# Fourier mixing and softmax attention on one core: the first product of a chain without its wait, and one reciprocal per full block of row sums

## The chip, the cores and the metric

The kernel runs on one core of one Trainium2 chip. The metric is the device time of one execution in microseconds (us); lower is better. One execution was also taken by the hardware profiler, and all lines below that come from the trace belong to that one.

## What is computed

The input `x` has 2048 rows of 512. The result mixes two things row by row with a gate `g = sigmoid(sum(x * gate_w))`:

```
a = Cr @ (x @ Hr.T) - Ci @ (x @ Hi.T)          # Fourier part, dense matrices: 2048x2048 and 512x512
p = softmax(q @ k.T * scale)                    # 32 heads of 16, 2048 x 2048 scores each
b = (p @ v) @ wo
out = g * a + (1 - g) * b
```

Here `q`, `k`, `v` come from a second input by one projection. All is float32. The kernel splits an operand into a high and a low part and makes three products (high·high, high·low, low·high) where one would lose accuracy.

## The kernel before, in words

**Stages.** (1) Projections for `q`, `k`, `v` and the imaginary hidden transform, whole array (128 rows). (2) One long stage in which attention and the Fourier part run side by side. (3) A tail: the last attention units, the last output projections and stores.

**Two streams side by side in stage 2.** The TensorE array has 128 rows. A matmul of the Fourier part (a "product", `Chain.mm`, L339 to L345) contracts over 128, but in this stage it is cut in two halves of 64 rows. While one half of the array computes a product, the other half computes a score matmul, since a score contracts over only 48 or 50 rows (16 per head, times three parts, and two rows that carry the negated maximum). So the list of products is issued twice per pair of segments: once for `half=0` and once for `half=1`, both adding into the same PSUM tile `d`.

- Score matmuls are of two kinds. An "a" score (`a_tile`, L198; matmul at L204) is made to find the row maximum: VectorE reduces it (L206). An "s" score (`scores`, L621; matmul at L629) is made transposed and goes through the exponential on ScalarE (L630) into a tile `pt`. Each kind has three PSUM buffers (`psA`, `psS`), so the fourth score of a kind waits until the first has been consumed.
- "Value" products (`pv`, L632; matmul at L638) multiply `pt` with `v` into the PSUM tile `acc`: four matmuls per unit, 17 columns each, in four column groups of the array. They need the exponentials of both heads of the unit. There are 512 units (16 head pairs x 32); row 16 of each group holds the sum of the exponentials.

**Chains.** A chain (`Chain`, L332) is all products that add into one tile `d`. There is one PSUM buffer for `d` in this stage (`psD`), so a new chain's first product must also wait until the chain before has been evacuated: ScalarE copies it at L359 (chains of 12, the real hidden transform), L397 or L400 (chains of 48, the sequence transform), or VectorE finishes it at L521 (chains of 9, the output projection). The evacuation is issued right behind the last product of the second half.

**Order of the work.** It is written out by hand. `pairs` (L764) yields pairs of segments, and `segment` (L738) walks through a pattern string. A slot of one letter issues one product, then one score of that kind on the other half of the array. A slot of two letters issues two scores and no product. A bar issues one unit of values. The patterns are

```python
FULL = "a s a s a s s a s a s a s a s a | |"
THIN = "aS s s a a s a | a s a a s s sA |"
NINE = "sA s s a a sA | a a s a s aS |", "aS a s s a aS | sA a s a s s sA |"
```

There are 13 pairs of THIN (12 products each, one chain per pair), 96 pairs of FULL (16 products each, one chain in three pairs) and 13 pairs of NINE (9 products each, one chain per pair). Ahead of them three chains are run with the whole array.

**The wait that is touched.** `users` collects who consumes each score issued since the last product of a segment (an exponential for "s", a reduction for "a"). At the next segment's start the list becomes `before`, and the first product of that segment gets a wait (L754) on the latest "s" consumer in it, or, if there is none, on the first entry. A FULL segment ends with one "a", so the next waits for its reduction. A THIN or NINE segment ends with scores of both kinds, so the next waits for its last exponential. The first pair of THIN starts with an empty list.

**Row sums.** Eight blocks (`hf` 0 or 1, `ct` 0 to 3) of up to four head pairs are normalised in passing. `sums` (L438) loads the sums of the exponentials from DRAM into `rc`, head 0 in partitions 0 to 63 and head 1 in 64 to 127, 64 elements in each; `inverse` (L446), put by the plan some units later, takes the reciprocals on VectorE (L450) and stores each half to DRAM (L451); `load_o` (L453) reads them back spread over rows. Seven blocks are full (`n` = 4); the block `hf` 1, `ct` 3 has three pairs. `run_plan` calls these ahead of a segment, so on each engine they stand in the queue ahead of that segment's work.

Of the kernel before, what the change touches and what calls it, by code (L numbers as in the profile page):

```python
# [31 lines left out]
def mix_kernel(ctx: ExitStack, tc: tile.TileContext, xa_t, xa, wqkv, w_hid, w_seq, wo, gate_w, out):  # L32
# [5 lines left out]
    nc = tc.nc  # L38
# [406 lines left out]

    def inverse(hf, ct, n=4):  # L446
        rc = rcs.pop((hf, ct))
        for h in range(2):
            rows = rc[64 * h:64 * h + 16 * n]
            nc.vector.reciprocal(rows, rows)  # L450
            nc.sync.dma_start(r_d[hf][ct][h, :n].rearrange("p (c f) -> c p f", f=64), rows)  # L451

    def load_o(o, sm, hf, ct, q0, n=4):  # L453
# [205 lines left out]
    def issue(x, half, stop=True):  # L659
        chain, st, mv, after, last = x  # L660
        i = chain.mm(st, mv, half, last and stop)
        if stop and after:
            after()
        return i
# [15 lines left out]
    for hf in range(2):  # L680
        for ct in range(4):
            n = 3 if hf and ct == 3 else 4
            last = 32 * (4 * ct + n - 1) + 16 * (hf + 1)
            at(last + (4 if ct < 3 else 2), sums, hf, ct, n)
            at(last + (12 if ct < 3 else 4), inverse, hf, ct, n)
            if ct < 3:
                for half in range(2):
                    for step, du in enumerate((16, 20, 22)):
                        at(last + du + 8 * half, block, step, hf, ct, half)
# [38 lines left out]
    def score(kind, h):  # L728
        x = next(streams[h][kind == "a"], None)
        if x:  # L730
            users.append((kind, (a_tile if kind == "a" else scores)(*x)))

    def values():
        nonlocal valued
        pv(valued)
        valued += 1

    def segment(pattern, half, ds, stop):  # L738


        nonlocal users
        before, users = users, []
        ds = iter(ds)
        for slot in pattern.split():
            if slot == "|":
                values()
                continue
            if len(slot) == 1:
                x = next(ds, None)
                if x:  # L750
                    i = issue(x, half, stop)
                    users = []
                    if before:
                        tc.add_manual_dep(  # L754
                            i.ins, dict(before).get("s", before[0][1]).ins.name,
                            mybir.DependencyInfo(mybir.DependencyClass.Sync, mybir.DependencyReason.DATA))
                        before = None
            score(slot[0], 1 - half)
            if len(slot) == 2:
                score(slot[1].lower(), half)  # L760
        if deferred:
            deferred.pop(0)()
# [29 lines left out]
    for patterns, ds in pairs():  # L792
        for half in range(2):
            run_plan(valued)
            segment(patterns[half], half, ds, half == 1)
# [59 lines left out]
```

## Time and profile before

| what | value |
|---|---|
| times of 3 runs | 1752.32 to 1754.02 us, median 1752.51 us |
| the profiled execution: its own time | 1753.26 us |
| the profiled execution: span from first to last instruction | 1751.5 us |
| mean granted TensorE clock in it | 0.995 |
| busy share: TensorE matmuls, VectorE, ScalarE, GpSimd | 99%, 78%, 66%, 26% |

In the lines of the profile PE is the matmul side of TensorE and PEld its weight loads; DVE is VectorE, ACT is ScalarE, POOL is GpSimd, SPq the queue of SyncE, which issues most DMAs. A timeline row gives the start in us from the span's start, the length in us, the engine, the source line, the operation, "output<-inputs", the shapes, and how many such instructions are merged in the row; in brackets stands how long the engine had been idle before it and what released it. Matmuls overlap: the length of one is longer than its distance to the next. A row of waits gives the total in us, the number of waits and the longest.

### The profile page before, as it was taken

To read this page: it belongs to the slowest core of one execution; us is meant where nothing else is said; L and a number is where in the kernel's file an instruction comes from. 1 tells how busy PE (TensorE), PEld (TensorE's weight loads), DVE (VectorE), ACT (ScalarE), POOL (GpSimd) and SP (SyncE) were. 2 spreads that over 40 slices of the span, in tenths; PEclk is the share of its full clock that TensorE was granted. 3 is DMA by queue.
4 is the path that set the end of the run, shared out by engine and by line. 5 is a ranking of instruction groups with operands and counts; after the bars stand their busy time and mean duration, and the time that the engine had idled before them with its cause. 6 is when DMAs were issued, how large, how long until landed. Compare 5 with 4: busy or idle time off the path is not lost.

```text
span 1751.5 us, 32890 instructions
## 1 busy us (share of the span) xinstructions
PE 1727.6 (99%) x12721; PEld 1042.1 (59%) x12721; DVE 1368.1 (78%) x2302; ACT 1153.6 (66%) x2257; POOL 447.0 (26%) x561
## 2 busy tenths in 40 slices
PE   8999999999999999999999999999999999999998
PEld 7886554456666666656666666666666566544443
DVE  5228878888888888888888888888888888899953
ACT  5211267776776777776767777767767777777776
POOL 0110222232223233222223243333323333200111
PEclk9999899999999999999999999999999999999999
DMA  8754630304133152414146443314141535461113
GB/s 291 234 113 138 224 42 7 56 21 78 44 62 67 45 123 80 86 55 79 38 80 211 107 127 98 72 57 86 44 85 56 129 98 98 146 168 26 38 27 127
DMA packets 82348, 164.79 MB, mean 94 GB/s; under 512 B 19712, under 2 KB 19968, under 8 KB 78352
## 3 DMA queue, kind: packets, MB, share of 16 engines
q1 hardware_dynamic: 77840, 162.30, 36.4%
q8 instruction: 100, 1.64, 0.4%
q0 software_dynamic: 4352, 0.39, 0.3%
q14 instruction: 56, 0.46, 0.1%
HBM read 107.47 MB, written 54.52 MB: 92 GB/s over the span
## 4 chain that ended last, share of the span: by engine, by line
PE 93%; DVE 2%; ACT 2%; DMA 1%; issue 0%; DVEq 0%; SPq 0%; ACTq 0%
PE d L343 35%; PE acc L638 26%; PE s L629 11%; PE a L204 11%; PE s L79 2%; PE s L80 2%; PE s L81 2%; DVE mx L206 1%; ACT pt L630 1%; DMA b<-hl 1%; PE a L79 1%; PE a L80 1%; PE a L81 1%; ACT y L359 0%; DVE hl L76 0%
## 5 line engine op out<-in xcount | busy, mean ns | idle before, releaser
L206 DVE TENSOR_REDUCE mx<-a 128x1 f32<-128x512 f32 x2026 | 1244.4, 681 | 243.3 <-PE a L204 229.5
L630 ACT ACTIVATE pt<-s 128x512 f32<-128x512 f32 x2008 | 1025.5, 622 | 391.2 <-PE s L629 333.7
L204 PE MATMUL a<-ks,qs 48*128 48x512 f32 x2026 | 814.4, 418 | 3.1 <-DVE mx L206 2.4
L629 PE MATMUL s<-qs,ks 50*128 50x512 f32 x2008 | 769.7, 413 | 0.9 <-ACT pt L630 0.8
L343 PE MATMUL d<-xab,ch 64*128 64x512 f32 x2016 | 648.7, 396 | 0.0
L638 PE MATMUL acc<-pt,vt 128*17 128x512 f32 x4096 | 500.3, 596 | 0.0
L343 PEld LDWEIGHTS d<-xab,ch 64*128 64x128 f32 x2016 | 365.9, 184 | 126.3 <-DVE mx L206 60.4
L629 PEld LDWEIGHTS s<-qs,ks 50*128 50x128 f32 x2008 | 365.6, 184 | 109.1 <-ACT pt L630 30.8
L204 PEld LDWEIGHTS a<-ks,qs 48*128 48x128 f32 x2026 | 366.8, 185 | 77.2 <-DVE mx L206 48.4
L343 PE MATMUL d<-xab,cl 64*128 64x512 f32 x1008 | 399.5, 396 | 0.0
L343 PEld LDWEIGHTS d<-xab,cl 64*128 64x128 f32 x1008 | 185.5, 184 | 64.9 <-DVE mx L206 40.8
L327 POOL CAST ch<-craw 128x512 fp32r<-128x512 f32 x126 | 77.1, 612 | 555.2 <-PE a L204 177.6
L638 PEld LDWEIGHTS acc<-pt,vt 128*17 128x17 f32 x4096 | 90.1, 96 | 206.0 <-issue 206.0
L328 POOL TENSOR_TENSOR cl<-craw,ch 128x512 fp32r<-128x512 f32 x126 | 162.1, 1287 | 10.2
L227 POOL DMA_DIRECT2D qs<-mt x128 | 72.0, 568 | 160.1 <-DVE mt L223 151.6
L343 PE MATMUL d<-wre,xab 64*128 64x512 f32 (+1 forms) x348 | 95.1, 406 | 5.0 <-ACT pt L630 2.5
L343 PEld LDWEIGHTS d<-wre,xab 64*128 64x128 f32 (+1 forms) x348 | 59.9, 185 | 42.6 <-issue 26.1
L343 PE MATMUL d<-wo_hl,o_hl 64*128 64x512 f32 (+1 forms) x261 | 71.0, 398 | 0.0
L343 PEld LDWEIGHTS d<-wo_hl,o_hl 64*128 64x128 f32 (+1 forms) x261 | 47.1, 185 | 15.9 <-issue 11.7
L75 ACT CAST hl<-s 128x512 fp32r<-128x512 f32 x32 | 18.7, 585 | 56.8 <-PE s L81 49.5
L76 DVE TENSOR_TENSOR hl<-s,hl 128x512 fp32r<-128x512 f32 x32 | 22.0, 687 | 35.0 <-ACT hl L75 35.0
L218 POOL CAST nhl<-nm 128x16 fp32r<-128x16 f32 x32 | 6.3, 197 | 151.2 <-DVE nm L215 151.2
(125 smaller groups left out, 931.8 us busy)
## 6 DMA issues: line engine op xcount, KB each, us to landing
craw<-w_seq SPq DMA_DIRECT2D x128, 256.0 KB
qk<-hl SPq DMA_DIRECT2D x32, 512.0 KB
qs<-qk SPq DMA_DIRECT2D x96, 128.0 KB
ks<-qk SPq DMA_DIRECT2D x96, 128.0 KB
b<-hl SPq DMA_DIRECT2D x16, 512.0 KB
xab<-b SPq DMA_DIRECT2D x16, 512.0 KB
o<-oe SPq DMA_DIRECT2D x62, 128.0 KB
oh<-nh SPq DMA_DIRECT2D x12, 512.0 KB
```

Of the source, the lines that this page charges most:

```text
L79: nc.tensor.matmul(ps, sh, mh, start=first, stop=False)
L80: nc.tensor.matmul(ps, sh, ml, start=False, stop=False)
L81: nc.tensor.matmul(ps, sl, mh, start=False, stop=last)
L204: nc.tensor.matmul(ps, qs[p % 2][r, qt * P:(qt + 1) * P], ks[p % 2][r, kb * 512:(kb + 1) * 512], start=True, stop=True)
L206: user = nc.vector.tensor_reduce(mx[p % 2][:, h, qt, kb:kb + 1], ps, AX.X, ALU.max)
L227: (nc.sync, nc.gpsimd)[h].dma_start(rows.rearrange("v (q b c) -> v b q c", q=8, b=4)[:, b], mt[hf][32 * b + h:32 * b + 32:2])
L327: nc.gpsimd.tensor_copy(h1, raw)
L328: nc.gpsimd.tensor_tensor(l1, raw, h1.bitcast(F32), ALU.subtract)
L343: i = nc.tensor.matmul(self.ps, st[r], mv[r], start=not self.begun, stop=stop)
L629: nc.tensor.matmul(ps, ks[p % 2][rr, kt * P:(kt + 1) * P], qs[p % 2][rr, q0:q0 + 512], start=True, stop=True)
L630: return nc.scalar.activation(pts[u][:, 2 * qb + h], ps, AF.Exp, bias=0.0, scale=DH ** -0.5)
L638: nc.tensor.matmul(acc[32 * j:32 * j + 17], vt[:, kt, p, 16 * h:16 * h + 17], pt[:, j], start=kt == 0, stop=kt == NT - 1)
```

## The change

Two edits. In `segment`, the list `before` is dropped when the product about to be issued is the first of its chain (`x[0].begun` is still false), so that product gets no wait on a score's consumer. Since the list is looked at only for the first product of a segment, this concerns segments in which a chain begins; the second segment of each pair, and the FULL pairs in the middle of a chain, keep their wait. In `inverse`, a full block takes one reciprocal over all 128 partitions of `rc` instead of two over 64 each; the block with three pairs keeps two operations. The two stores stay as they are.

```diff
     def inverse(hf, ct, n=4):
         rc = rcs.pop((hf, ct))
+        if n == 4:
+            nc.vector.reciprocal(rc, rc)
         for h in range(2):
             rows = rc[64 * h:64 * h + 16 * n]
-            nc.vector.reciprocal(rows, rows)
+            if n < 4:
+                nc.vector.reciprocal(rows, rows)
             nc.sync.dma_start(r_d[hf][ct][h, :n].rearrange("p (c f) -> c p f", f=64), rows)
...
                 x = next(ds, None)
                 if x:
+
+                    before = before if x[0].begun else None
                     i = issue(x, half, stop)
                     users = []
                     if before:
```

## The prediction

> **What bounds the kernel now.** First the page: the shares of the chain that ended last, by engine.
>
> ```profile
> PE 93%; DVE 2%; ACT 2%; DMA 1%; issue 0%; DVEq 0%; SPq 0%; ACTq 0%
> ```
>
> TensorE holds 93% of the chain. An edit that leaves TensorE's order of work alone can save only what TensorE stands still for, and the change takes away waits of TensorE. So the second view is the table of stages, here THIN's and FULL's (columns: window, length, PE busy, PEld, DVE, ACT, POOL, clock, DMA share, GB/s).
>
> ```profile
> 217.00:389.00 172.00, 169.38 (x1220) 83.84 (x1220) 141.70 (x233) 125.53 (x240) 40.24 (x53) 1.00 0.20 33
> 389.00:1532.00 1143.00, 1141.74 (x9208) 705.00 (x9212) 947.62 (x1597) 811.39 (x1606) 352.64 (x437) 1.00 0.36 86
> ```
>
> TensorE lacks 2.6 us of full in THIN's stage and 1.3 us in FULL's. There is little to win. The third view is who waited: matmuls, then weight loads.
>
> ```profile
> PE d L343 <- ACT pt L630: 3.3, 13, 0.7
> PEld d L343 <- DVE mx L206: 102.1, 120, 0.9
> PEld d L343 <- issue: 54.1, 66, 2.8
> ```
>
> The first row is a real stop: 13 times the array ran dry before a product, released by an exponential. The second looks far larger, 102 us, and is the trap of this profile: the weight load path also "waits" as long where nothing releases it (third row), as the next part shows.
>
> **The change, part by part.** From the loops, a chain begins 13 times in THIN, 32 times in FULL, 13 times in NINE; the first THIN start has no wait to lose. So 57 waits go: 12 THIN, the first FULL start (behind THIN), 31 FULL, 13 NINE.
>
> *31 FULL starts.* One of them, with what stands before it:
>
> ```profile
> 424.07 0.77 ACT L397 ACTIVATE y<-d,g 128x512 f32<-128x512 f32 x1
> 424.18 0.68 DVE L206 TENSOR_REDUCE mx<-a 128x1 f32<-128x512 f32 x1
> 424.41 1.04 PE L638 MATMUL acc<-pt,vt 128*17 128x512 f32 x8
> 425.38 0.50 PE L343 MATMUL d<-xab,ch 64*128 64x512 f32 x1
> 425.39 0.50 PE L204 MATMUL a<-ks,qs 48*128 48x512 f32 x1
> ```
>
> The removed wait is on the reduction that ends at 424.86; the product starts at 425.38, 0.52 us later and 0.97 us after the last eight value products began. A segment's middle, where this wait never was:
>
> ```profile
> 349.09 1.05 PE L638 MATMUL acc<-pt,vt 128*17 128x512 f32 x8
> 350.07 0.18 PEld L343 LDWEIGHTS d<-wre,xab 64*128 64x128 f32 x1 [0.85 <-issue]
> 350.07 0.50 PE L343 MATMUL d<-wre,xab 64*128 64x512 f32 x1
> 350.41 0.39 PE L343 MATMUL d<-wre,xab 64*128 64x512 f32 x1
> ```
>
> Again 0.98 us, with 0.85 us "idle" on the load path and nothing to release it. So the step from values to products costs the same with or without the wait: the value products hide it, with 0.52 us to spare, and I cost these 31 at nothing. The evacuation also ends at 424.84, no later than the reduction. If the cover were gone (value products half a microsecond shorter), the reduction would bind.
>
> *13 NINE starts.* Here a pair of scores comes first and the product second:
>
> ```profile
> 1600.19 1.05 PE L638 MATMUL acc<-pt,vt 128*17 128x512 f32 x8
> 1601.17 0.50 PE L629 MATMUL s<-qs,ks 50*128 50x512 f32 x1
> 1601.52 0.40 PE L343 MATMUL d<-wo_hl,o_hl 64*128 64x512 f32 x1
> ```
>
> The scores come 0.98 us after the values, the product 0.35 us after them. The unhindered second slot above is 350.41 − 350.07 = 0.34 us behind the first. Nothing to win.
>
> *12 THIN starts.* Same pattern, but the product is late:
>
> ```profile
> 351.36 0.39 PE L629 MATMUL s<-qs,ks 50*128 50x512 f32 x1
> 351.59 0.47 PE L629 MATMUL s<-qs,ks 50*128 50x512 f32 x1
> 352.97 0.49 PE L204 MATMUL a<-ks,qs 48*128 48x512 f32 x1
> 353.69 0.49 PE L343 MATMUL d<-wre,xab 64*128 64x512 f32 x1 [0.22 <-ACT pt L630]
> 354.02 0.39 PE L343 MATMUL d<-wre,xab 64*128 64x512 f32 x1
> 355.28 1.12 PE L638 MATMUL acc<-pt,vt 128*17 128x512 f32 x8
> ```
>
> 0.72 us instead of 0.34: 0.38 us late. ScalarE in the same stretch:
>
> ```profile
> 352.06 0.58 ACT L359 COPY y<-d 128x512 f32<-128x512 f32 x1
> 352.53 1.11 ACT L630 ACTIVATE pt<-s 128x512 f32<-128x512 f32 x2
> 353.02 1.12 ACT L630 ACTIVATE pt<-s 128x512 f32<-128x512 f32 x2
> 354.23 1.08 ACT L630 ACTIVATE pt<-s 128x512 f32<-128x512 f32 x2
> ```
>
> (The second and third row share one exponential.) The evacuation pushes the exponentials of the scores at 351.36 and 351.59 back; the second ends at 352.53 + 1.11 = 353.64, and the product starts right behind. Without the wait it goes at 352.97 + 0.34 = 353.31, since `d` is free at 352.64; the score beside it needs the buffer of the one at 351.36, free at about 353.14, and goes along. What is late next? The second score needs the buffer of the one at 351.59, free at 353.64. It takes the place that the first score has today, so the score stream gains one slot, 354.02 − 353.69 less the 0.10 us longer first step, 0.23 us. And the values at 355.28 need the exponentials of these two scores, which end at 354.23 + 1.08 = 355.31 today; the eight values then take 1.12 us instead of 1.05, so they already wait for them. ScalarE starts queued exponentials 0.49 us apart (352.53, 353.02), and each lasts 1.11 − 0.49 = 0.62. The third began 0.62 before its end at 354.14, at 353.52; the fourth, now at 354.23, could follow 0.50 later, at 354.02. ScalarE gives 0.20 us, and I take that: 12 x 0.20 = 2.4 us. Bounds: 0, if more of ScalarE's backlog comes back than I see, and the whole 0.38 us, 4.6 us in all. A loss is excluded by the queue's order, which stays, unless rival (4) holds.
>
> *The first FULL start*, behind THIN:
>
> ```profile
> 387.93 1.05 PE L638 MATMUL acc<-pt,vt 128*17 128x512 f32 x8
> 388.00 0.58 ACT L359 COPY y<-d 128x512 f32<-128x512 f32 x1
> 389.71 0.47 PE L343 MATMUL d<-xab,chl 64*128 64x512 f32 x1 [0.73 <-ACT pt L630]
> ```
>
> Unhindered it is 387.93 + 0.98 = 388.91, with `d` free at 388.58. That is 0.8 us. Its partner is an "a", and reductions are not behind; the next "s" comes a slot later and needs a buffer that has been freed long before. I take 0.8 us, between 0 and 0.8.
>
> *Reciprocals.* VectorE, with the shapes that bear on the price:
>
> ```profile
> L450 DVE RECIPROCAL rc<-rc 64x64 f32<-64x64 f32 x14 | 7.4, 529 | 3.0 <-DMA rc<-o 2.7
> L450 DVE RECIPROCAL rc<-rc 48x64 f32<-48x64 f32 x2 | 1.1, 542 | 0.0
> ```
>
> 48 partitions cost no less than 64 do, so the price goes by the elements per partition, and one over 128x64 is taken at 0.53 us; the other bound is twice that, what the two cost now. Two in one FULL segment show as
>
> ```profile
> 592.51 3.68 DVE L206 TENSOR_REDUCE mx<-a 128x1 f32<-128x512 f32 x6 [0.94 <-PE a L204]
> 597.42 1.08 DVE L450 RECIPROCAL rc<-rc 64x64 f32<-64x64 f32 x2
> 598.54 4.87 DVE L206 TENSOR_REDUCE mx<-a 128x1 f32<-128x512 f32 x8
> 604.48 1.89 DVE L206 TENSOR_REDUCE mx<-a 128x1 f32<-128x512 f32 x3 [1.07 <-PE a L204]
> ```
>
> From 592.51 to 598.54 are 6.03 us, from there to 604.48 are 5.94, the usual segment: VectorE has about 1.0 us of room in a segment, and the pair overruns it by 0.09. One operation fits. By the plan six of the seven full blocks fall into FULL: 6 x 0.09 = 0.5 us, between 0 and 0.5. The seventh falls into the tail. There one operation waits for both loads, and the first store goes out after it, some 0.7 us later than now:
>
> ```profile
> 1705.49 1.24 DVE L450 RECIPROCAL rc<-rc 64x64 f32<-64x64 f32 x2 [2.66 <-DMA rc<-o]
> 1719.23 1.23 DVE L488 TENSOR_TENSOR o_l<-o_raw,o_l 128x1024 fp32r<-128x1024 f32 x1
> 1724.55 0.50 PE L343 MATMUL d<-wo_hl,o_l 128*128 128x512 f32 x1
> ```
>
> In SP's queue these stores are followed by the reads of the same sums, which wait for them anyway. What is made of them is ready at 1720.46 and used first at 1724.55: 4.1 us of slack for 0.7. Nothing.
>
> **Sum:** 2.4 + 0.8 + 0.5 = 3.7 us. The profiled execution took 1753.26 us around its span of 1751.5, so 1749.6; the median of the runs is 0.75 us below the profiled one: 1752.51 − 3.7 = **1748.8 us**, 0.21% less. A measurement of this kernel can tell about 0.2% (3.5 us) from no change, so my forecast lies on that line.
>
> **The rivals.**
> (1) *TensorE keeps all it gains in THIN*: exponentials come sooner than I think and the 0.38 us stay, 2.2 us more off (12 x 0.18), 1746.6. For it: ScalarE is busy 73% of that stage. Against: the values' 1.12 us.
> (2) *FULL starts gain too*: the first product's weights load under the value products once nothing holds it, and its 0.50 us shrink to 0.39: 31 x 0.11 = 3.4 us more off, 1745.4. Against: at 350.07, without a wait, the load still starts with its product. The Trainium skill, "TensorE: Matmul & The Clock Gate", Step-by-step: what each phase is for, says that TensorE pulls weight loads ahead of running matmuls when the row groups don't conflict or a background buffer takes them; by that rule this rival would hold, and the row at 350.07 speaks against it at this place.
> (3) *THIN gives it all back* to ScalarE before the pair ends: 0.8 + 0.5 = 1.3 us, 1751.2.
> (4) *The starts lose step* (slower): the wait kept product and score side by side. If the score's buffer comes free over one slot (0.23 us) after the product, the product runs alone, and at the 31 FULL and 13 NINE starts a slot is lost: 44 x 0.23 = 10.1, less the 3.7: 6.4 us above the median, 1758.9. Against: the "a" at 425.39 leaves with its product, and its buffer was freed two reductions before 424.86.
> (5) *Nothing changes*, because the release of `d` holds the product anyway: 1752.5. Against: 352.64 and 388.58 are well before the products.
>
> **How the numbers follow.** Forecast 0.61, (1) 0.12, (2) 0.07, (3) 0.10, (4) 0.08, (5) 0.02. The forecast's half beyond the line is 0.31, so faster by over 0.2% is 0.31 + 0.12 + 0.07 = 0.50, within it 0.30 + 0.10 + 0.02 = 0.42, slower 0.08. The range takes in the bounds of THIN (0 to 4.6), of the first FULL start and of the reciprocals, so it reaches from rival (1) to a little past rival (3): 1746.6 to 1751.8. It leaves out (2), (4) and (5), 0.17.
>
> **What would show it.** In the changed profile the row of matmul waits for an exponential should fall from 13 to about one or none; a THIN start should put its product 0.34 us behind the first scores, with the second score held until an exponential ends; the values behind it should come about 0.2 us sooner; the first FULL product should come 0.98 us after the eight values; the other FULL starts should keep 0.97 us; segments with a reciprocal should last 5.94 us. I am wrong if FULL's usual segment changes its length, if a product at a chain's start runs without its score, or if the tail stretches.

## The result, and the profile after

Over 20 runs of each kernel the changed kernel took 1751.03 us (median; 1748.23 to 1755.13) and the kernel before 1753.76 us. The ratio is 0.998, with a 95% interval from 0.9973 to 0.9987. So the change gains 0.2% by this ratio, and 2.7 us (0.16%) between the medians; the forecast's line of 0.2% lies inside the interval. The forecast had 3.7 us off. The time forecast, 1748.8 us, lies 2.2 us below the one measured; 1.25 us of that is the kernel before, whose median in these 20 runs is that much above the 1752.51 us from which the forecast started.

The profiled execution after spans 1748.6 us (1751.5 before) and took 1750.4 us around it. First the chain of work that ended last, and from the waits of matmuls one row that is new (who waited for whom, total in us, times, longest):

```profile
PE 95%; DVE 2%; DMA 1%; ACT 1%; issue 0%; POOL 0%; DVEq 0%; SPq 0%; ACTq 0%; POOLq 0%
```

```profile
PE s L632 <- DMA qs<-mt: 1.2, 1, 1.2
```

TensorE's share of the chain rose from 93% to 95%. The row of 13 products that waited for an exponential, 3.3 us, is gone; the new row comes up again below. (Scores, exponentials and values now stand at L632, L633 and L641.) What is not gone with it shows only in the lengths of segments, so all that follows measures from a segment's first product to the next one's.

*THIN starts.* A start in the profile after, TensorE and ScalarE together:

```profile
350.16 3.08 ACT L633 ACTIVATE pt<-s 128x512 f32<-128x512 f32 x6
350.61 0.73 PE L632 MATMUL s<-qs,ks 50*128 50x512 f32 x2
350.95 0.64 PE L343 MATMUL d<-wre,xab 64*128 64x512 f32 x2
351.32 0.50 PE L632 MATMUL s<-qs,ks 50*128 50x512 f32 x1
352.68 1.16 PE L641 MATMUL acc<-pt,vt 128*17 128x512 f32 x8
```

The product follows the scores by 350.95 − 350.61 = 0.34 us, where it was 0.72. The values follow them by 2.07 us, where it was 355.28 − 352.97 = 2.31; the eight values then last 0.04 us longer. The first products of the second and the thirteenth THIN pair, before and then after, are eleven pairs apart:

```profile
245.79 0.50 PE L343 MATMUL d<-wre,xab 64*128 64x512 f32 x1 [0.20 <-ACT pt L630]
...
377.66 0.49 PE L343 MATMUL d<-wre,xab 64*128 64x512 f32 x1 [0.21 <-ACT pt L630]
```

```profile
244.87 0.64 PE L343 MATMUL d<-wre,xab 64*128 64x512 f32 x2
...
374.53 0.64 PE L343 MATMUL d<-wre,xab 64*128 64x512 f32 x2
```

131.87 / 11 = 11.99 us a pair became 129.66 / 11 = 11.79, so 0.20 us a start.

*First FULL start.* It comes 0.98 us after the eight values, as anywhere else:

```profile
384.98 1.05 PE L641 MATMUL acc<-pt,vt 128*17 128x512 f32 x8
385.96 0.49 PE L343 MATMUL d<-xab,chl 64*128 64x512 f32 x1
```

*A reciprocal in FULL.* VectorE after:

```profile
593.81 0.51 DVE L449 RECIPROCAL rc<-rc 128x64 f32<-128x64 f32 x1
594.84 4.88 DVE L206 TENSOR_REDUCE mx<-a 128x1 f32<-128x512 f32 x8 [0.52 <-PE a L204]
```

One operation over 128 partitions takes 0.51 us, and VectorE now stands idle 0.52 us before the next reduction. The six segments concerned last 5.943 us on the mean, 6.032 before.

*The other FULL starts.* This is where the forecast put nothing. One segment in which a chain begins, before (its first product starts at 425.38, a row of the prediction) and then after, with the loads on PEld:

```profile
425.93 4.87 DVE L206 TENSOR_REDUCE mx<-a 128x1 f32<-128x512 f32 x8 [1.07 <-PE a L204]
429.06 0.18 PEld L204 LDWEIGHTS a<-ks,qs 48*128 48x128 f32 x1
429.49 1.91 PE L638 MATMUL acc<-pt,vt 128*17 128x512 f32 x16
431.33 0.50 PE L343 MATMUL d<-xab,ch 64*128 64x512 f32 x1
```

```profile
421.64 0.50 PE L343 MATMUL d<-xab,ch 64*128 64x512 f32 x1
422.21 4.88 DVE L206 TENSOR_REDUCE mx<-a 128x1 f32<-128x512 f32 x8 [1.09 <-PE a L204]
425.35 0.18 PEld L204 LDWEIGHTS a<-ks,qs 48*128 48x128 f32 x1
425.78 1.91 PE L641 MATMUL acc<-pt,vt 128*17 128x512 f32 x16
427.62 0.50 PE L343 MATMUL d<-xab,ch 64*128 64x512 f32 x1
```

From the first product to the first reduction: 0.55 us before, 0.57 after. To the last "a" load: 3.68 and 3.71. To the values: 4.11 and 4.14. To the next segment: 5.95 and 5.98. The segment is 0.025 us longer (medians 5.947 and 5.971 us over 30 chain starts; the segments in which no chain begins stay at 5.947).

*Where the 2.9 us between the two spans come from*, each as a difference of distances between first products:

| stretch | change, us |
|---|---|
| up to THIN's first product (233.53 to 232.96; no edit there) | −0.57 |
| 12 THIN starts | −2.36 |
| first FULL start (last THIN half 6.24 to 5.42) | −0.82 |
| six segments behind a reciprocal, 6 x 0.089 | −0.53 |
| 30 other FULL starts (their sum 178.44 to 179.16) | +0.72 |
| four segments at FULL's end (24.96 to 25.61) | +0.65 |
| rest of FULL | +0.17 |
| NINE (150.69 to 150.65) and tail (67.42 to 67.35) | −0.11 |

The +0.65 sits at one score, after and then before:

```profile
1508.57 0.47 PE L632 MATMUL s<-qs,ks 50*128 50x512 f32 x1 [1.22 <-DMA qs<-mt]
```

```profile
1511.31 0.47 PE L629 MATMUL s<-qs,ks 50*128 50x512 f32 x1 [0.55 <-ACT pt L630]
```

It waits for a small transfer of the negated maxima, whose last part GpSimd issues at 1503.30 us. In the eleven further kernels below, these four segments last between 24.66 and 25.59 us with no order by the edits: the kernel with all of the wait edit and nothing else has 24.87. I read it as scatter of that transfer between executions, not as an effect of the change.

### The profile page after: what moved, and what is told of

Its sections match the earlier page's. It is cut to its first block, busy times and chain, and to the rows that moved or that the text cites. A ratio compares the mean times of both kernels' runs of the same rounds, so it can differ in the third digit from the quotient of the medians.

```text
span 1748.6 us, 32869 instructions
## 1 busy us (share of the span) xinstructions
PE 1726.6 (99%) x12721; PEld 1041.4 (60%) x12721; DVE 1364.2 (78%) x2295; ACT 1152.2 (66%) x2257; POOL 447.9 (26%) x561
## 4 chain that ended last, share of the span: by engine, by line
PE 95%; DVE 2%; DMA 1%; ACT 1%; issue 0%; POOL 0%; DVEq 0%; SPq 0%; ACTq 0%; POOLq 0%
PE d L343 34%; PE acc L641 27%; PE a L204 12%; PE s L632 12%; PE s L79 2%; PE s L80 2%; PE s L81 2%; DVE mx L206 1%; PE a L79 1%; PE a L80 1%; PE a L81 1%; DMA b<-hl 1%; ACT pt L633 0%; PE a L343 0%; DMA qs<-mt 0%
## 5 line engine op out<-in xcount | busy, mean ns | idle before, releaser
L633 ACT ACTIVATE pt<-s 128x512 f32<-128x512 f32 x2008 | 1024.1, 620 | 390.0 <-PE s L632 342.3
L632 PE MATMUL s<-qs,ks 50*128 50x512 f32 x2008 | 769.9, 413 | 1.5 <-DMA qs<-mt 1.2
L641 PE MATMUL acc<-pt,vt 128*17 128x512 f32 x4096 | 500.7, 596 | 0.0
L632 PEld LDWEIGHTS s<-qs,ks 50*128 50x128 f32 x2008 | 366.1, 184 | 112.0 <-ACT pt L633 33.6
L641 PEld LDWEIGHTS acc<-pt,vt 128*17 128x17 f32 x4096 | 90.6, 96 | 205.8 <-issue 205.7
```

The costliest lines, as they stand in the source:

```text
L632: nc.tensor.matmul(ps, ks[p % 2][rr, kt * P:(kt + 1) * P], qs[p % 2][rr, q0:q0 + 512], start=True, stop=True)
L633: return nc.scalar.activation(pts[u][:, 2 * qb + h], ps, AF.Exp, bias=0.0, scale=DH ** -0.5)
L641: nc.tensor.matmul(acc[32 * j:32 * j + 17], vt[:, kt, p, 16 * h:16 * h + 17], pt[:, j], start=kt == 0, stop=kt == NT - 1)
```

## The experiments

The theory from these profiles: dropping the wait gains 0.20 us at each THIN start and 0.8 us at the first FULL start, and loses 0.025 us at every other FULL start. Rivals: the longer FULL segments come from the reciprocal edit or from a drift of the work, or from the moment at which the product starts. A loss of 0.7 us is under what whole runs can tell, so the segment lengths decide; the ratios stand beside them. All figures in us; 5.947 is a segment with no chain start.

| kernel | THIN pair | last THIN half | chain start in FULL | behind a reciprocal | NINE | ratio, 95% interval |
|---|---|---|---|---|---|---|
| before | 11.988 | 6.241 | 5.947 | 6.032 | 150.69 | |
| after | 11.788 | 5.420 | 5.971 | 5.943 | 150.65 | 0.998, 0.9973 to 0.9987 |
| wait edit alone | 11.788 | 5.417 | 5.971 | 6.029 | 150.69 | 0.9995, 0.9986 to 1.0005 |
| reciprocal alone | 11.989 | 6.230 | 5.946 | 5.946 | 150.69 | 0.9997, 0.9987 to 1.0006 |
| FULL starts keep the wait | 11.786 | 5.434 | 5.946 | 5.943 | 150.64 | 0.9981, 0.9972 to 0.9991 |
| FULL starts alone lose it | 11.980 | 6.220 | 5.971 | 6.031 | 150.62 | 1.0009, 0.9995 to 1.0023 |
| earlier reduction | 11.789 | 5.416 | 5.944 | 5.943 | 150.76 | 0.998, 0.9969 to 0.999 |
| evacuation on VectorE | 11.796 | 5.632 | 5.970 | 5.944 | 150.64 | 0.9986, 0.9977 to 0.9995 |
| one reciprocal for three pairs | 11.792 | 5.417 | 5.945 | 5.945 | 149.90 | 0.9987, 0.9978 to 0.9995 |
| score first | 11.798 | 5.420 | 5.932 | 5.944 | 150.63 | 0.9986, 0.9977 to 0.9996 |
| later values | 12.036 | 5.431 | 5.970 | 5.944 | 150.67 | 1.0009, 0.9999 to 1.0019 |
| score first, three pairs | 11.787 | 5.417 | 5.933 | 5.945 | 149.90 | 0.9981, 0.9972 to 0.999 |
| the same with later values | 12.037 | 5.430 | 5.935 | 5.946 | 149.82 | 1.0, 0.9991 to 1.0008 |

"Last THIN half" is the distance from the last THIN half's first product to FULL's first.

**The wait edit alone**, on the kernel before:

```diff
                 if x:
+                    before = before if x[0].begun else None
                     i = issue(x, half, stop)
```

> The wait dropped at all chain starts, the two reciprocals kept as before. Theory A: the edit gains 12 x 0.20 us at the THIN starts and 0.8 us at the first FULL start, and loses about 0.025 us at each of 31 FULL starts, since the first product now signals its own end ahead of its score and the first reduction starts later; so 2.4 us less than before, a FULL segment that begins a chain lasts 5.972 us, the others 5.947, and the six segments with two reciprocals stay at 6.03. Rival B: the longer chain-start segments have to do with the reciprocal edit or are drift; then they last 5.947 here and the gain is 3.2 us.

The span was 1749.1 us. THIN and the first FULL start gain as in the changed kernel and the other FULL starts lose as in it. One of them:

```profile
422.29 0.50 PE L343 MATMUL d<-xab,ch 64*128 64x512 f32 x1
422.86 4.88 DVE L206 TENSOR_REDUCE mx<-a 128x1 f32<-128x512 f32 x8 [1.09 <-PE a L204]
428.27 0.50 PE L343 MATMUL d<-xab,ch 64*128 64x512 f32 x1
```

Again 0.57 us to the first reduction and 5.98 us in all. Segments behind a reciprocal keep their 6.03 us. So the loss does not come from the reciprocals.

**The reciprocal alone**, the change without its second edit:

```diff
-                    before = before if x[0].begun else None
                     i = issue(x, half, stop)
```

> The waits kept as before, one reciprocal per full block. Theory A: six segments lose 0.09 us each, 0.5 us in all, too little for the times to tell; a FULL segment that begins a chain lasts 5.947 us like the others. Rival B: those segments last 5.972 us here. Rival C: the tail or the stores of the sums pay something back, and the stage behind FULL gets longer by a few tenths of a us.

Only the six segments move. The span of 1753.8 us is longer than before's; 3.0 us of that lie ahead of THIN (236.57 against 233.53), where nothing was edited. The last section comes back to this stretch.

**FULL starts keep the wait.** The change, but a list without an "s" is kept:

```diff
-                    before = before if x[0].begun else None
+                    before = before if x[0].begun or "s" not in dict(before or ()) else None
```

> The change, but the wait stays where it is on a reduction (31 FULL starts and the first NINE start). Theory A: the gains stay and the loss goes: 2.4 + 0.8 + 0.5 = 3.7 us less than before, 0.8 us less than the change itself; chain-start segments at 5.947 us. Rival B: chain-start segments stay at 5.972 us and the time is that of the change. The stall of the score behind the late transfer near the end of FULL (0.84 us in the profile before, 1.49 in the one after) may fall either way; theory A takes it for jitter that no edit moves.

```profile
423.00 0.50 PE L343 MATMUL d<-xab,ch 64*128 64x512 f32 x1
423.54 4.88 DVE L206 TENSOR_REDUCE mx<-a 128x1 f32<-128x512 f32 x8 [1.07 <-PE a L204]
428.94 0.50 PE L343 MATMUL d<-xab,ch 64*128 64x512 f32 x1
```

0.54 and 5.94 us: with the wait on the reduction back, the loss is gone, and the gains in THIN stay.

**FULL starts alone lose it**, on the kernel before:

```diff
+                    before = before if x[0].begun or "s" in dict(before or ()) else None
                     i = issue(x, half, stop)
```

> The wait dropped only where it is on a reduction (31 FULL starts, the first NINE start), reciprocals as before. Theory A: slower than before by 31 x 0.025 = 0.8 us, chain-start segments at 5.972 us, THIN pairs unchanged at 11.99 us. Rival B: no change in any segment, the time is that of before. Rival D, that the wait did cost something in FULL: up to 0.1 us less at each start, 3 us faster.

```profile
430.64 0.50 PE L343 MATMUL d<-xab,ch 64*128 64x512 f32 x1
431.21 4.88 DVE L206 TENSOR_REDUCE mx<-a 128x1 f32<-128x512 f32 x8 [1.10 <-PE a L204]
436.62 0.50 PE L343 MATMUL d<-xab,ch 64*128 64x512 f32 x1
```

0.57 and 5.98 us with nothing else changed: this part of the change costs time by itself. The ratio's interval does not exclude 1, as is to be expected of 0.7 us.

**An earlier reduction.** Is it the moment of the start, or that the product carries a wait at all? Here the product at a FULL start waits for the reduction two places earlier, which has long ended:

```diff
+            if kind == "a":
+                reduced.append(users[-1])
...
-                    before = before if x[0].begun else None
+                    if before and not x[0].begun:
+                        before = None if "s" in dict(before) else reduced[-3:-2]
```

> The change, but at the 31 FULL starts the first product waits for the reduction that frees the buffer of the score beside it, two reductions earlier than the wait of before. Theory A (what costs 0.025 us is that the score now carries a wait of its own, so the product in front of it has to signal its own end and the score's signal comes 0.026 us later): the score needs no wait of its own, the signals are merged again, chain-start segments at 5.947 us, the time as in the run that keeps the wait. Rival E (the late wait itself kept something in step that runs ahead without it): an earlier wait holds nothing, so 5.972 us as in the change.

```profile
422.22 0.49 PE L343 MATMUL d<-xab,ch 64*128 64x512 f32 x1
422.76 4.87 DVE L206 TENSOR_REDUCE mx<-a 128x1 f32<-128x512 f32 x8 [1.07 <-PE a L204]
428.16 0.49 PE L343 MATMUL d<-xab,ch 64*128 64x512 f32 x1
```

0.54 and 5.94 us. A wait that never holds anything up makes the segment shorter. So it matters where the wait stands, not how long it waits. The semaphore events of the trace, at the second chain in FULL, say what moves. Before, and in this kernel, the "a" at a segment's start has no wait of its own on VectorE: the product ahead of it has one already, and covers it. Product and "a" then tell VectorE of their ends in one signal, 518 ns (here 517) after the product's start. After the change the load of the "a" carries the wait for its buffer itself, the product has to signal its own end first, at 511 ns, and the signal of the "a" comes at 545. VectorE's first reduction moves with it, from a median of 542 ns to 568.

The kernel before shows the same without any edit. At three of its 30 chain starts (639.60, 925.21 and 1210.86 us) the load of the "a" has a wait of its own anyway, on a semaphore that transfers raise. There product and "a" signal one by one, the first reduction starts 566 to 569 ns after the product, and the segments last 5.968 to 5.975 us. The change lengthens the other 27 from 5.945 us on the mean to 5.972, which is all of the 0.72 us; the three stay as they were.

The 26 ns reach the segment's end because VectorE's reductions are part of its loop. They run 0.598 us apart, and the load of the last "a" goes right behind the end of the fifth, which frees its buffer: before, 0.54 + 4 x 0.598 + 0.68 + 0.07 = 3.68 us after the start; then 0.43 us to the values and 1.84 us to the next product make 5.95. The Trainium skill ("TensorE: Matmul & The Clock Gate", The cost: per-tile semaphore tail) says that completion signals of packed matmuls are written one after the other, some 26 ns each. Here the signal of the "a" comes 27 ns later, at 545 instead of 518, with one signal more, which agrees.

**Score first.** If signals are what counts, issuing the score ahead of the product should help. At FULL starts without a wait:

```diff
+                    swap = before and not x[0].begun and "s" not in dict(before)
                     before = before if x[0].begun else None
+                    if swap:
+                        score(slot[0], 1 - half)
+                        first_user = users[-1]
                     i = issue(x, half, stop)
...
-            score(slot[0], 1 - half)
+            if len(slot) == 1 and x and swap:
+                users.append(first_user)
+            else:
+                score(slot[0], 1 - half)
```

> The change, but at the 31 FULL starts the score is issued ahead of the chain's first product; each keeps its own waits. Theory A (what counts is that the product signals ahead of the score): the score signals first, the first reduction starts as early as before, chain-start segments at 5.947 us. Rival E (something runs ahead without the late wait): 5.972 us as in the change.

```profile
422.43 0.49 PE L204 MATMUL a<-ks,qs 48*128 48x512 f32 x1
422.43 0.49 PE L343 MATMUL d<-xab,ch 64*128 64x512 f32 x1
422.96 4.87 DVE L206 TENSOR_REDUCE mx<-a 128x1 f32<-128x512 f32 x8 [1.06 <-PE a L204]
428.36 0.50 PE L343 MATMUL d<-xab,ch 64*128 64x512 f32 x1
```

The score signals at 506 ns, the first reduction starts at a median of 530, and the segment lasts 5.932 us: shorter than before the change by 0.015. First reductions at 530, 542 and 568 ns go with segments of 5.932, 5.947 and 5.971 us: the segment follows the reduction almost one for one.

**Evacuation on VectorE.** The prediction let ScalarE's backlog, pushed up by the evacuation, set what a THIN start gains. Then taking that copy off ScalarE should gain about as much again:

```diff
-        nc.scalar.copy(y, chain.ps)
+        nc.vector.tensor_copy(y, chain.ps)
```

> The change, with the evacuation of the THIN chains moved from ScalarE to VectorE. Theory A (a THIN start keeps only 0.20 of the 0.38 us because ScalarE is behind by the evacuation and the values wait for its exponentials): ScalarE is no longer behind, so a THIN pair falls from 11.79 to about 11.6 us, provided VectorE, which gets 0.6 us more per pair, does not become late with reductions. Rival F (the rest is lost to the score buffers or to a restart of the array, not to ScalarE): the pair stays at 11.79 us. If VectorE gets late, the pair gets longer and the row of waits names its reductions.

This theory fell. The pair takes 11.796 us, no less. A start (TensorE, then ScalarE):

```profile
351.54 0.72 PE L632 MATMUL s<-qs,ks 50*128 50x512 f32 x2
351.88 0.39 PE L343 MATMUL d<-wre,xab 64*128 64x512 f32 x1
...
353.62 1.15 PE L641 MATMUL acc<-pt,vt 128*17 128x512 f32 x8
```

```profile
352.10 2.06 ACT L633 ACTIVATE pt<-s 128x512 f32<-128x512 f32 x4 [0.40 <-PE s L632]
```

ScalarE now stands idle 0.40 us and starts when the pair's first score is there, 0.56 us after it began. Three exponentials 0.49 us apart, the last 0.62 long, end 0.56 + 2 x 0.49 + 0.62 = 2.16 us after the scores (2.14 in the trace). The last of the unit's four value matmuls (each stands twice in the trace) waits for the third exponential: its load goes 2.18 to 2.20 us after the scores in all twelve such starts, here and in the changed kernel, and 2.37 to 2.39 before. The first value matmul does come sooner without the backlog, after 1.87 to 1.88 us in nine of the twelve starts (2.07 to 2.08 in the other three, of which this is one), where the changed kernel has 2.06 to 2.07. That gains nothing, for the product behind the values follows the scores by 3.15 to 3.16 us in both. In the changed kernel ScalarE's queue of six from 350.16 reaches the pair's first score at 350.16 + 2 x 0.49 = 351.14, just when that score is there (350.61 + 0.56 = 351.17). So the pair's own scores set the end of the start, and the backlog has been worked off by then. Only the first FULL start is later here, by 0.21 us (5.632 in the table): its product waits for VectorE's copy of `d`.

**Later values.** Could the values simply come a slot later, behind another product and an "a"? In the first half of each THIN pair:

```diff
     THIN = "aS s s a a s a | a s a a s s sA |"
+    LATE = "aS s s a a s a a | s a a s s sA |"
...
-            yield (THIN,) * 2, take(hid, 12)
+            yield (LATE, THIN), take(hid, 12)
```

> The change, with the first bar of the first segment of a THIN pair one slot later (one product and one a-score from behind the values to ahead of them). Theory G, formed on the run with VectorE's evacuation: a THIN start keeps only part of its 0.38 us because the values wait for the exponentials of the pair's own first scores, which ScalarE cannot end earlier than about 2.15 us after the first score; with one slot more in front, the values no longer wait, and a pair falls from 11.79 by about 0.1 us, to 11.69. Rival H (reductions or score buffers hold the segment): the pair stays at 11.79 or gets longer, and the row of waits names reductions.

The pair is 0.25 us longer. The values no longer wait, but the "a" moved ahead of them does. Its load in this kernel, and the waits of such loads in THIN (window 245 to 389), in this kernel and then in the changed one:

```profile
356.52 0.18 PEld L204 LDWEIGHTS a<-ks,qs 48*128 48x128 f32 x1 [0.52 <-DVE mx L206]
```

```profile
PEld a L204 <- DVE mx L206: 26.6, 36, 0.9
```

```profile
PEld a L204 <- DVE mx L206: 19.6, 23, 0.9
```

These loads wait 7.0 us more for reductions in twelve pairs, of which 12 x 0.25 = 3.0 us show in the pairs. ScalarE's bound at a THIN start has VectorE's right behind it.

**One reciprocal for three pairs.** The block with three pairs keeps two operations of 0.54 us, and in NINE VectorE has less room. Here they become one, over 112 partitions, and the FULL starts keep their wait:

```diff
+        if n < 4:
+            nc.gpsimd.memset(rc, 1.0)
...
-        if n == 4:
-            nc.vector.reciprocal(rc, rc)
+        nc.vector.reciprocal(rc[:64 + 16 * n], rc[:64 + 16 * n])
```

> The version with the wait kept in FULL, and also one reciprocal over 112 partitions for the block of three pairs, with the rows between set to one beforehand. Theory A (VectorE's room per segment is what counts): the NINE segment around 1663 us, 6.66 us before and after, falls by up to 0.5 us, since one operation of 0.55 us goes; in all 4.2 us less than before, 1.3 us less than the change. Rival: that segment is late for another reason, the transfer that the reciprocal waits for or the reductions in front of it, and stays at 6.66 us.

The operation in this kernel, and the two in the changed one, each with the reductions behind it:

```profile
1661.86 0.54 DVE L450 RECIPROCAL rc<-rc 112x64 f32<-112x64 f32 x1
1662.32 2.41 DVE L206 TENSOR_REDUCE mx<-a 128x1 f32<-128x512 f32 x4
```

```profile
1660.94 1.12 DVE L453 RECIPROCAL rc<-rc 48x64 f32<-48x64 f32 x2
1662.09 2.48 DVE L206 TENSOR_REDUCE mx<-a 128x1 f32<-128x512 f32 x4
```

NINE takes 149.90 us instead of 150.64, all of it in the segment behind the reciprocal (6.66 to 5.90). That is more than the operation that is saved lasts (0.55 us). The next reduction starts 1.15 us after the first of two reciprocals, and 0.46 us after a single one, whose end it overlaps: 0.69 us sooner. The load of an "a" waits for the end of that reduction, 1.90 us after the reciprocal's start in the changed kernel and 1.14 here.

**Together.** The kernel with the score first gets the one reciprocal in the block of three as well:

```diff
+        if n < 4:
+            nc.gpsimd.memset(rc, 1.0)
...
+        nc.vector.reciprocal(rc[:64 + 16 * n], rc[:64 + 16 * n])
```

> The change with the score ahead of the product at the 31 FULL starts, and one reciprocal for the block of three pairs too. From the segments measured so far: 2.4 + 0.8 + 0.5 as in the change, 31 x 0.015 = 0.5 us from the FULL starts, 0.75 us in NINE: 4.9 us less than before, a ratio of about 0.997; FULL starts 5.932 us, the NINE segment around 1663 us at 5.90. Rival: the two do not add, because an earlier start of FULL meets the late transfer at its end and waits the longer.

And the same with the later values on top:

```diff
-            yield (THIN,) * 2, take(hid, 12)
+            yield (LATE, THIN), take(hid, 12)
```

> The same with the later bar in THIN. Theory G: 1.2 us less than that, 6.1 us less than before, a ratio of about 0.9965. Rival H: no better than without the later bar.

The first has the shortest span of all, 1746.9 us, and a median of 1749.85 us against 1753.57 for the kernel before beside it. The gains add up: 5.933 us at FULL starts and 149.90 in NINE, as in the kernels that have one of them. From THIN's first product to the end it takes 5.3 us less than the kernel before (1746.9 − 234.27 against 1751.5 − 233.53), and 3.0 us less than the changed kernel; 0.8 us of these are the late transfer's. It is the version to keep, but by its ratio, 0.9981 (0.9972 to 0.999), it can't be told from the change. The second loses what the later values lose, 0.25 us a pair.

## Why the prediction was right, and where it was wrong

- **THIN starts, 12 x 0.20 us:** right in size (2.36 us), and in its signs: the product 0.34 us behind the scores, the second score held a little, the values sooner by about 0.2. The reason was wrong in part. ScalarE does set it, but not by its backlog behind the evacuation: the experiment with the evacuation on VectorE took the backlog away, and the pair got no shorter. The floor is the pair's own first scores and three exponentials in line. That 0.20 came out either way is partly luck.
- **First FULL start, 0.8 us:** right (0.82).
- **Reciprocals, 6 x 0.09 us:** right (0.089 each). One operation over 128 partitions lasts 0.51 us where 0.53 was taken. That it would go by the elements in a partition was more than the rows told, as all had 64; they show that it does not rise with the partitions.
- **31 FULL starts "at nothing":** this is the step that failed. The next product does come 0.97 us behind the values, as said, and the wait was hidden there. But the working asked only what the product waits for, and not which later instruction its wait also covers or who waits for the signals. With the wait gone from the product, the score beside it needs its own, the first reduction starts 26 ns later, and 27 of the segments lose 0.72 us together, which is a fifth of what the other steps gain. The forecast named another length of FULL's usual segment as a sign that it was wrong: the usual segment kept its 5.947 us, and those in which a chain begins changed.
- **13 NINE starts and the tail, nothing:** right (−0.04 and −0.07 us).
- **The rivals.** TensorE keeping 0.38 us in THIN: no, the exponentials took 0.18 back. The weight load going ahead at FULL starts: no, the first load there still starts with its product, at 421.64. THIN giving all back: no. Starts losing step: there is a loss at the FULL starts on account of the product and score side by side, but of 0.025 us and not a slot of 0.23, and by another mechanism; product and score still leave together. Nothing at all: no.

The sum with the failed term put right is 3.7 − 0.7 = 3.0 us, against 2.7 between the medians.

## What to carry to other kernels

Before a wait is removed from an instruction, ask which later instruction on the same engine it also covered: the wait moves there, the instruction in front has to signal its own end, and whoever consumes the result starts later. Where that consumer's queue is part of the loop (here eight reductions back to back), tens of nanoseconds come back once per turn, though the engine shows 78% busy. And an edit below what whole runs can tell is decided by distances between like instructions inside one trace, over many turns.

## What the runs showed that was not expected

*The stretch before THIN differs more between executions than all edits together.* THIN's first product came at 232.96 us in the changed kernel's profile and at 238.81 in that of the kernel in which FULL starts alone lose the wait, though both are the same up to there. The window 160 to 240 us of the changed kernel and of that one, and 1680 to 1740 us of the kernel in which FULL starts keep the wait (third figure from the end: granted clock):

```profile
160.00:240.00 80.00, 73.27 (x316) 45.29 (x316) 60.03 (x115) 24.48 (x46) 17.77 (x19) 0.96 0.65 194
```

```profile
160.00:240.00 80.00, 71.82 (x274) 44.75 (x275) 55.21 (x108) 20.36 (x38) 17.40 (x19) 0.89 0.66 195
```

```profile
1680.00:1740.00 60.00, 59.07 (x350) 27.10 (x351) 18.58 (x32) 46.84 (x95) 7.79 (x9) 0.97 0.19 54
```

In the clock's records the granted clock falls to half for 3.4 us or a multiple of it: 6.8 and 17.1 us in the first two windows, which gives their 0.96 and 0.89; and once in the tail of the third kernel, which then lasted 68.9 us instead of 67.4. The Trainium skill ("TensorE: Matmul & The Clock Gate", What's actually happening) has a clock of full or half speed set by a free-running window of 3413 ns, and the 3.4 us agree. Three such windows more came with 5.85 us here, twice what the change gains. What sets a window to half stays open: in the third kernel TensorE was busy for 3.18 of the 3.40 us ahead of it. Whole runs go with the granted clock: of the 91 runs of the kernel before beside the experiments, 43 at a mean of 0.996 took 1752.8 us on the mean and five at 0.992 took 1758.3. So the ratios are uncertain by 0.1%, and the segments were compared instead.

*A reciprocal's price does not rise with the partitions.* 48, 64, 112 and 128 partitions of 64 elements took between 0.50 and 0.55 us.
